# Reordering the first loads and tile preparations of a fused LayerNorm, linear-attention and GELU-MLP kernel

## The chip, the cores and the metric

The kernel runs on one core of a Trainium2 chip. The metric is the device time of one execution in microseconds (us), and I quote medians of several executions. A "span" is the length of one profiled execution, from its first to its last instruction; it is 1.7 to 1.9 us shorter than the time. A load has "landed" when its semaphore is full, which is when the engine that waits for it goes on (quarter 0 of W1 lands at 6.65 us and the matmul that waits for it starts at 6.69); the "pitch" of matmuls is the time from one start to the next. The engines are TensorE (PE in the profile, with its weight loads as PEld), VectorE (DVE), ScalarE (ACT), GpSimd (POOL) and SyncE (SP), which issues most of the DMAs.

## The reference

```python
x = A_x                                    # (1, 2048, 640) bf16
xn = layernorm(x)                          # eps 1e-5, no affine part
# A: linear attention with 32 heads of 20
q, k, v = split(xn @ wqkv)                 # wqkv 640 x 1920
phi = lambda t: where(t > 0, t + 1, exp(t)) + 1e-6
kv = einsum(phi(k), v); z = phi(k).sum(tokens)
attn = (phi(q) @ kv / (phi(q) @ z + 1e-6)) @ wo
# B: MLP
mlp = gelu(xn @ w1 + b1) @ w2 + b2         # w1 640 x 1536
return x + attn + mlp
```

Everything below concerns the first 21 us, in which the kernel computes xn for the first few of 16 tiles of 128 tokens and starts on xn @ w1.

## The kernel before

The kernel records instructions per engine in program order, and adds a semaphore wait wherever data or a buffer demands it. An engine starts its instructions in the order of its own list: in the kernel before ScalarE copies tile 0's second piece at 6.51 us and the bias, which stands behind it in the list, at 6.90. The order in the source text therefore matters only within one engine: moving VectorE work past a TensorE unit in the text leaves both lists as they are.

The opening of the kernel before:

```python
# loads; W1 (640 x 1536) comes in four column quarters of 480 KB, x in tiles of 160 KB
dma_x(0, 1)
dma_w("scalar", b1tmp[:], ...)      # bias, on ScalarE's queue
dma_w1(0, "scalar")                 # quarter 0, on ScalarE's queue
dma_x(1, 1); dma_w1(1); dma_x(2, 1); dma_w1(2); dma_x(3, 1); dma_w1(3)   # SyncE's queue
dma_x(4, 2); dma_x(6, 2); ...
# ... (cut)
filler(10)                          # ten zero matmuls of 512 columns
ln_stats(0)                         # VectorE: statistics of tile 0
ln_half(1, 0); ln_half(1, 1); ln_aggr(1)
norm0(0, CA, r_xnA)                 # tile 0 normalised in two pieces: columns 0-255
norm0(CA, D, r_xnB)                 # and 256-639
dA, sA, bA = transp0(0, 2, r_xnA)   # TensorE transposes into PSUM
filler(1)
dB, sB, bB = transp0(2, DT, r_xnB)
# VectorE copies the first piece out of PSUM, ScalarE the second
b1_step()                           # bias transposed on TensorE, copied by ScalarE
ln_norm(1)
h_first([0, 1, 2])                  # first useful matmuls: quarter 0, first piece then second
# ... (cut)
xnT_copy(1, transp(1))
ln_stats(2)
ln_next(2)                          # statistics of tile 3, THEN norm of tile 2
units(0, 1, 3, 2 * JQ)              # units(t0, n, lo, hi): n tiles of tokens, 128-column
units(1, 1, 0, 2 * JQ)              # blocks lo..hi-1 of W1; JQ = 3 blocks are a quarter
units(0, 2, 2 * JQ, 2 * JQ + 2)
xnT_copy(2, transp(2))
units(0, 2, 2 * JQ + 2, JT)
ln_next(3)
ln_next(4)
units(2, 1, 0, JQ)
xnT_copy(3, transp(3))
units(2, 1, JQ, JT)                 # one tile wide: matmuls of 128 columns
units(3, 1, 0, JT)
# tiles 4 to 15 are transposed by DMA; then units of 2 and 4 tiles
```

A normalisation is a chain over three engines: statistics (VectorE, two halves), aggregate (VectorE), the power -0.5 (GpSimd), normalise (VectorE), transpose (TensorE), copy (VectorE or ScalarE). A "unit" means five accumulating matmuls and one GELU.

## Time and profile before

| | before |
|---|---|
| time, median of 3 | 210.07 us (209.99 to 210.41) |
| span of the profiled execution | 207.9 us |
| TensorE busy | 203.1 us, 98% |
| granted TensorE clock | 1.000 |

Part 1 of the page gives busy time and share by engine; part 4 gives the engines' shares of the chain that ended last.

```profile
PE 203.1 (98%) x1592; PEld 140.4 (68%) x1598; DVE 108.1 (52%) x226; ACT 74.3 (36%) x141; POOL 21.1 (10%) x59
...
PE 91%; DVE 4%; DMA 3%; issue 1%; ACTq 0%; DVEq 0%
```

TensorE is the bottleneck nearly throughout. The start of the chain, in order of time (start, length, what), says what TensorE waited for first:

```profile
1.45 5.20 DMA W<-in_B_w_dram
6.65 0.05 issue
6.69 1.04 PE ps L382 x15
7.74 0.28 PE ps L336 x5
8.02 3.60 PE ps L352 x55
11.62 0.28 PE ps L336 x5
11.90 3.02 PE ps L352 x35
```

W1's quarter 0 is issued at 1.45 us and lands at 6.65; from then on the chain is TensorE without a break (the lines behind 14.92 us are cut). The timeline of TensorE for the same stretch (start, length, engine, line, operation, tiles, form, count, and idle time before it with what ended it) shows the same from the engine's side:

```profile
5.72 0.28 PE L372 MATMUL ps<-ident,xn_tm 128*128 128x128 bf16 x2 [0.57 <-DVE xn_tm L365]
5.84 0.38 PE L295 MATMUL ps<-warm 128*128 128x512 bf16 x1
6.14 0.34 PE L372 MATMUL ps<-ident,xn_tm 128*128 128x128 bf16 x3
6.41 0.18 PE L300 MATMUL ps<-ident,b1tmp 12*128 12x12 bf16 x1
6.69 1.04 PE L382 MATMUL ps<-xnT,W 128*128 128x128 bf16 x15
7.57 0.44 PE L336 MATMUL ps<-ident,xn_tm 128*128 128x128 bf16 x5
7.85 3.77 PE L352 MATMUL ps<-xnT,W 128*128 128x128 bf16 x55
```

L382 is the first useful matmul. L336 are the transposes of tiles 1 to 3. Behind 7.57 no idle time is noted: a change of this stretch can pay only by starting TensorE's work earlier or by making it shorter.

### The profile page before, as it was taken

The numbers are of one execution on the slowest core, as the hardware profiler recorded it, in microseconds if no ns is written. First come the engines' busy times: TensorE is split into PE (matmuls) and PEld (weight loads), VectorE is DVE, ScalarE is ACT, GpSimd is POOL, SyncE is SP. The second block draws the span as 40 slices with busy tenths as digits, with TensorE's granted clock in tenths as the row PEclk, the third lists the DMA queues.
The fourth block names the chain that finished last, engine by engine and source line by source line (L and its number), as shares of the span: only waits on it lengthen the run. The fifth ranks groups of instructions, "written<-read, shape, count | busy, mean of one in ns | idle before, by whom it ended". The sixth has DMA issues, their size and how long they took to land.

```text
span 207.9 us, 3963 instructions
## 1 busy us (share of the span) xinstructions
PE 203.1 (98%) x1592; PEld 140.4 (68%) x1598; DVE 108.1 (52%) x226; ACT 74.3 (36%) x141; POOL 21.1 (10%) x59
## 2 busy tenths in 40 slices
PE   7899999999999999999999999999999999999995
PEld 2799886444457777777756565577777777777775
DVE  4689960000008888998268865474863422523322
ACT  2689887666676445111153577100000000000000
POOL 3245567000041000000000000000000000000000
PEclk9999999999999999999999999999999999999999
DMA  5999779997000000000000000681111111001001
GB/s 167 343 358 110 119 123 152 372 324 249 3 0 0 0 3 0 0 3 0 0 3 2 0 3 0 202 309 47 71 59 57 63 39 54 32 32 35 32 34 62
DMA packets 22698, 17.98 MB, mean 86 GB/s; under 512 B 9240, under 2 KB 22680, under 8 KB 22680
## 3 DMA queue, kind: packets, MB, share of 16 engines
q1 hardware_dynamic: 22000, 17.24, 29.5%
q10 hardware_dynamic: 680, 0.49, 0.9%
q8 instruction: 12, 0.20, 0.4%
q14 instruction: 6, 0.05, 0.1%
HBM read 12.62 MB, written 2.62 MB: 73 GB/s over the span
## 4 chain that ended last, share of the span: by engine, by line
PE 91%; DVE 4%; DMA 3%; issue 1%; ACTq 0%; DVEq 0%
PE ps L612 33%; PE ps L352 25%; PE ps L511 10%; PE ps L473 10%; PE ps L523 7%; DVE PQ L463 3%; DMA W<-in_B_w_dram 3%; PE ps L648 2%; DVE ek L461 1%; PE ps L532 1%; PE ps L548 1%; PE ps L558 1%; PE ps L382 1%; PE ps L336 0%; ACTq L233 0%
## 5 line engine op out<-in xcount | busy, mean ns | idle before, releaser
L352 PE MATMUL ps<-xnT,W 128*128 128x128 bf16 (+2 forms) x432 | 51.8, 281 | 0.2
L612 PE MATMUL ps<-W,HG 128*128 128x320 bf16 x360 | 51.0, 299 | 0.0
L352 PEld LDWEIGHTS ps<-xnT,W 128*128 128x128 bf16 x435 | 35.5, 98 | 15.6
L612 PEld LDWEIGHTS ps<-W,HG 128*128 128x128 bf16 x360 | 35.1, 98 | 14.2 <-issue 0.4
L356 ACT ACTIVATE HG<-ps,b1c 128x128 bf16<-128x128 f32 (+2 forms) x87 | 40.0, 492 | 12.5 <-PE ps L352 10.3
L461 DVE TENSOR_SCALAR ek<-ek 128x512 bf16<-128x512 bf16 (+1 forms) x36 | 11.1, 308 | 41.7 <-ACT ek L460 40.5
L460 ACT ACTIVATE ek<-ps 128x512 bf16<-128x512 f32 (+1 forms) x36 | 23.2, 644 | 19.8 <-PE ps L523 10.1
L631 DVE TENSOR_TENSOR out_sb<-ps,xnT 128x640 bf16<-128x640 f32 x15 | 12.4, 825 | 33.5 <-PE ps L612 33.3
L612 PE MATMUL ps<-Msb,PQ 128*128 128x320 bf16 x150 | 22.3, 299 | 0.0
L511 PE MATMUL ps<-xPK,xn_tm 128*128 128x320 bf16 x160 | 22.1, 299 | 0.0
L473 PE MATMUL ps<-Wqkv,xnT 128*128 128x320 bf16 x160 | 21.9, 299 | 0.0
L523 PE MATMUL ps<-xnT,Wqkv 128*128 128x512 bf16 x97 | 21.4, 379 | 0.3 <-issue 0.2
L473 PEld LDWEIGHTS ps<-Wqkv,xnT 128*128 128x128 bf16 x160 | 15.6, 98 | 6.3
L511 PEld LDWEIGHTS ps<-xPK,xn_tm 128*128 128x128 bf16 x160 | 15.6, 98 | 6.0
L612 PEld LDWEIGHTS ps<-Msb,PQ 128*128 128x128 bf16 x150 | 14.6, 98 | 5.7
L523 PEld LDWEIGHTS ps<-xnT,Wqkv 128*128 128x128 bf16 x100 | 11.6, 118 | 9.6 <-ACT Msb L553 0.2
L463 DVE SCALAR_TENSOR_TENSOR PQ<-ps,ek 128x512 bf16<-128x512 f32 x20 | 13.8, 692 | 2.1
L308 DVE BATCH_NORM_STATS2 stats<-xPK 128x6 f32<-128x320 bf16 x32 | 13.6, 466 | 2.5 <-DMA xPK<-in_A_x_dram 2.4
L463 DVE SCALAR_TENSOR_TENSOR xPK<-ps,ek 128x640 bf16<-128x640 f32 x16 | 13.2, 825 | 1.7
L498 DVE TENSOR_TENSOR Msb<-Msb,xPK 128x640 f32<-128x640 f32 x14 | 11.6, 826 | 0.5
L515 ACT ACTIVATE W<-ps 128x640 bf16<-128x640 f32 x5 | 3.5, 703 | 18.6 <-PE ps L511 18.6
L318 POOL TENSOR_TENSOR rstd<-aggr,mhalf 128x1 f32<-128x1 f32 x16 | 9.1, 568 | 8.9 <-DVE aggr L316 8.9
(62 smaller groups left out, 90.6 us busy)
## 6 DMA issues: line engine op xcount, KB each, us to landing
xnT<-in_A_x_dram SPq DMA_DIRECT2D x4, 640.0 KB, 6.6
Wqkv<-in_A_wqkv_dram SPq DMA_DIRECT2D x3, 800.0 KB, 6.4
out_dram<-out_sb SPq DMA_DIRECT2D x15, 160.0 KB, 1.8
W<-in_B_w_dram SPq DMA_DIRECT2D x1, 1920.0 KB, 15.6
W<-in_B_w_dram SPq DMA_DIRECT2D x3, 480.0 KB, 6.8
xPK<-in_A_x_dram SPq DMA_DIRECT2D x2, 640.0 KB, 9.4
Wo<-in_A_wo_dram SPq DMA_DIRECT2D x1, 800.0 KB, 10.9
xPK<-in_A_x_dram SPq DMA_DIRECT2D x4, 160.0 KB, 4.2
```

The source lines that it names most:

```text
L308: Pl.ins(v, lambda e: e.bn_stats(stats[:, s, 6 * h:6 * h + 6], x_in[:, t, h * HW:(h + 1) * HW]), reads=[r_x[t]], writes=[r_stats[s][h]])
L352: Pl.ins("tensor", [(lambda e, k=k: e.matmul(bank(b, 0, w), W1[:, k, jb * P:(jb + 1) * P], xnT[:, k, tok], start=(k == 0), stop=(k == DT - ...
L356: Pl.ins("scalar", lambda e: e.activation(HG[:, jb, tok], bank(b, 0, w), ACT.Gelu_apprx_tanh, bias=b1c[:, jb:jb + 1]), reads=[B_[b], r_b1c ...
L460: Pl.ins("scalar", lambda e: e.activation(e2, src, ACT.Exp), reads=br, writes=[r_ek[s]])
L461: Pl.ins(v, lambda e: e.tensor_scalar(et, et, 1.0, 1e-6, ALU.min, ALU.add), reads=[r_ek[s]], writes=[r_ek[s]])
L463: Pl.ins(v, lambda e: e.scalar_tensor_tensor(out=d2, in0=src, scalar=0.0, in1=e2, op0=ALU.max, op1=ALU.add), reads=br + [r_ek[s]], writes= ...
L473: fns.append(lambda e, k=k, h=h, b=b, t=t: e.matmul(bank(b + h, 0, HW), xnT[:, k, t * P:(t + 1) * P], Wqkv[:, k, D + h * HW:D + (h + 1) * ...
L498: Pl.ins(v, lambda e, t=t: e.tensor_tensor(out=zsum, in0=zsum, in1=PK[:, t, :], op=ALU.add), reads=[r_PK[t], r_zsum], writes=[r_zsum])
L511: Pl.ins("tensor", [(lambda e, t=t, h=h, b=b, f=f: e.matmul(bank(b + h, 0, HW), xn_tm[:, t, f * P:(f + 1) * P], PK[:, t, h * HW:(h + 1) * ...
L523: Pl.ins("tensor", [(lambda e, k=k, j=j, b=b: e.matmul(bank(b), Wqkv[:, k, j:D:DT], xnT[:, k, cc], start=(k == 0), stop=(k == DT - 1))) fo ...
L612: return lambda e: e.matmul(bank(b + h, 0, HW), l, r[:, h * HW:(h + 1) * HW], start=(i == 0), stop=(i == JT + DT - 1))
L631: Pl.ins(v, lambda e: e.tensor_tensor(out=halves(out_sb[:, s, :]), in0=pair(b), in1=halves(x_res[:, t, :]), op=ALU.add), reads=B_[b:b + 2] ...
```

## The change

The intent: all of the first loads on one queue, in the order in which they are needed, so that quarter 0 is not shared against quarter 1; tile 0's normalisation ahead of tile 1's aggregate; the bias transpose out of the way among the zero matmuls; tile 2's normalisation no longer behind tile 3's statistics; and tiles 2 and 3 together in the second half of W1.

```diff
         dma_x(0, 1)
         dma_w("scalar", b1tmp[:], ...)
-        dma_w1(0, "scalar")
         dma_x(1, 1)
+        dma_w1(0)
         dma_w1(1)
+        dma_w1(2)
         dma_x(2, 1)
-        dma_w1(2)
+        dma_w1(3)
         dma_x(3, 1)
-        dma_w1(3)
 ...
-        filler(10)
+        filler(6)
+        b1_step()
+        filler(3)
         ln_stats(0)
         ln_half(1, 0)
         ln_half(1, 1)
-        ln_aggr(1)
         norm0(0, CA, r_xnA)
         norm0(CA, D, r_xnB)
+        ln_aggr(1)
 ...   (first piece now copied by ScalarE, second by VectorE)
-        b1_step()
         ln_norm(1)
         h_first([0, 1, 2])
 ...
         xnT_copy(1, transp(1))
-        ln_stats(2)
-        ln_next(2)
         units(0, 1, 3, 2 * JQ)
         units(1, 1, 0, 2 * JQ)
-        units(0, 2, 2 * JQ, 2 * JQ + 2)
+        units(0, 2, 2 * JQ, 3 * JQ)
+        ln_stats(2)
+        ln_norm(2)
+        ln_half(3, 0)
+        ln_half(3, 1)
+        ln_aggr(3)
         xnT_copy(2, transp(2))
-        units(0, 2, 2 * JQ + 2, JT)
-        ln_next(3)
+        units(0, 2, 3 * JQ, JT)
+        ln_half(4, 0)
+        ln_norm(3)
+        ln_half(4, 1)
+        ln_aggr(4)
+        units(2, 1, 0, JQ)
+        b3 = transp(3)
+        xnT_copy(3, b3)
+        units(2, 1, JQ, 2 * JQ)
         ln_next(4)
-        units(2, 1, 0, JQ)
-        xnT_copy(3, transp(3))
-        units(2, 1, JQ, JT)
-        units(3, 1, 0, JT)
+        units(3, 1, 0, 2 * JQ)
+        units(2, 2, 2 * JQ, JT)
```

In both kernels tile 1's transposes come right behind the first three units: in that place TensorE's order is the same.

More of the change, by code (lines that the diff above doesn't have):

```diff
@@ L403, in bass_parallel_sum__linear_attn_block__dense_activation_gelu__prompt_kernel @@
         dB, sB, bB = transp0(2, DT, r_xnB)
-        Pl.ins(v, lambda e: e.tensor_copy(dA, sA), reads=[B_[bA]], writes=[r_xnTA])
-        Pl.ins("scalar", lambda e: e.activation(dB, sB, ACT.Copy), reads=[B_[bB]], writes=[r_xnT[0]])
-        b1_step()
+        Pl.ins("scalar", lambda e: e.activation(dA, sA, ACT.Copy), reads=[B_[bA]], writes=[r_xnTA])
+        Pl.ins(v, lambda e: e.tensor_copy(dB, sB), reads=[B_[bB]], writes=[r_xnT[0]])
         ln_norm(1)
```

## The prediction

> **What bounds it now.** TensorE: busy 203.1 of 207.9 us (page, part 1), 91% of the chain that ended last, granted clock 1.000. In time order PE does filler until 5.1 us, waits for the first normalised tile, and starts its first useful matmul at 6.69 us. From 7.06 us to 115 us it never idles. So a change to the first 21 us pays only by what it brings forward PE's work from 7 us on, or makes that work shorter.
>
> **What holds the first matmuls (timeline, tile and DMA views).** W1 quarter 0, alone on ACT's queue, lands at 6.65 us; quarter 1 at 7.66, x2 8.10, quarter 2 9.61, x3 10.07, quarter 3 11.57. Nearly as late are tile 0's transposed halves: VectorE's copy ends at 6.33, ScalarE's at 7.00 (PE stalls a trace there: the second half starts at 7.06).
>
> **What the change does.**
> 1. DMA order. In 4.4-6.2 us both queues moved data together at 343 GB/s (DMA view by queue)[...]. Estimate from the landings: 6.0 us (issued 0.3 us later). Total bytes up to quarter 1 are unchanged, so it still lands at about 7.55. Later steady pace: 480 KB per 1.5 us, 160 KB per 0.45. So x2 moves back, to about 9.5 (was 8.10), x3 to 11.5 (was 10.07).
> 2. Tile 0. Its normalisation no longer waits behind tile 1's aggregate (0.27 us earlier); swapped copies: halves ready at about 6.2 and 6.6. First matmul about 6.25, second half 6.63 instead of 7.06: -0.43 us. The bias transpose (0.18 us) leaves a PE gap, worth nothing by itself.
> 3. Six 256-wide units replace twelve 128-wide ones. PE's pitch is 55.9 ns at 128 columns, 109.2 ns at 256: 60x55.9-30x109.2 = 0.08 us saved. ScalarE was within its pace: nothing.
> 4. VectorE work is reordered: tile 2 no longer waits for x3; norm(4) moves behind the third copy, so tile 4's DMA transpose goes out near 16.9 us (was 15.08), tile 5's near 18.2 (was 16.90), landing near 20.9 (was 19.49).
>
> **How much reaches PE.** The 0.43 is taken back in turns. Quarter 1 is needed at 7.41 and lands near 7.55: 0.25 left. Tile 2's transposes come up at about 11.75; from x2's landing through stats, aggregate, power and normalisation to PE is 2.46 us by the durations of tiles 0 and 1, so 9.5 gives about 11.97: a stall of 0.2, gain about zero. The later steps have slack. The merge leaves about 0.1. Tile 5's transpose lands at about the time (20.8-20.9) when PE asks for it, so up to 0.2 may go there. From there the program is the same.
>
> **Prediction.** 209.95 us, range 209.3 to 210.6. Faster by over 2%: 0.01; within 2%: 0.98; slower by over 2%: 0.01.
>
> **What would show it.** Step 1: landings of quarter 0 near 6.0, quarter 1 7.4-7.7, x2 9.3-9.7. Step 2: first useful matmul 6.2-6.3, its second half near 6.63. Gain taken back: small PE idle before the first 128-wide unit (DMA W) and before tile 2's transposes (VectorE xn_tm), and perhaps before the first unit of tiles 4-5 (DMA transpose). Step 3: that unit starts within 0.3 us of the earlier 20.90. The end, PE chain and DVE-bound stretch at 115-123 us, unchanged.
>
> **What would make it wrong.** If one queue fills the slow stretch at 2.8-4.3 us (213 GB/s), all loads land up to 0.5 us sooner and the gain of 0.4-0.5 survives. If quarter 0 lands after 6.6, or tile 5's transpose runs into the long stall that tile 6's showed (4.7 us to landing against 2.6), it loses 0.5-1.5 us.

The 6.0 us is quarter 0's landing, and an estimate: it takes quarter 0 to be through before quarter 1 starts, which no trace had shown. The sum is that of "How much reaches PE": of the 0.43 us 0.25 are left at quarter 1 and about none at tile 2's transposes; the merge brings about 0.1, and tile 5's transpose may take up to 0.2. It comes to about 0.1 us under the 210.07 of the kernel before, the 209.95 predicted.

## The result, and the profile after

| | before | after |
|---|---|---|
| time, median | 210.15 us (209.99 to 210.50, 6 runs) | 209.97 us (209.82 to 210.37, 6 runs) |
| ratio, 95% interval | | 0.9991 (0.9978 to 1.0004) |
| span of the profiled execution | 207.9 us | 208.5 us |
| granted TensorE clock | 1.000 | 1.000 |

A ratio is the mean time of one kernel's fast runs over that of the other's in the same rounds, so it is not quite the ratio of the medians. The time did not change clear of noise. The profiled span is 0.6 us longer than before, although the medians are 0.18 us shorter. The runs' own times settle most of that: the profiled execution of the kernel before took 209.68 us, less than all six runs of its median, and that of the changed kernel 210.37 us, the longest of its six.

Part 1 of the page, and TensorE's timeline of the changed kernel:

```profile
PE 204.2 (98%) x1567; PEld 139.7 (67%) x1567; DVE 108.5 (52%) x226; ACT 73.9 (35%) x135; POOL 21.4 (10%) x59
```

```profile
5.40 0.40 PE L372 MATMUL ps<-ident,xn_tm 128*128 128x128 bf16 x2
5.58 0.46 PE L295 MATMUL ps<-warm 128*128 128x512 bf16 x1
5.88 0.33 PE L372 MATMUL ps<-ident,xn_tm 128*128 128x128 bf16 x3
6.60 1.01 PE L382 MATMUL ps<-xnT,W 128*128 128x128 bf16 x15 [0.39 <-DMA W<-in_B_w_dram]
7.45 0.44 PE L336 MATMUL ps<-ident,xn_tm 128*128 128x128 bf16 x5
8.11 4.32 PE L352 MATMUL ps<-xnT,W 128*128 128x128 bf16 x60 [0.22 <-DMA W<-in_B_w_dram]
12.50 0.45 PE L336 MATMUL ps<-ident,xn_tm 128*128 128x128 bf16 x5
```

Tile 0's transposes start 0.3 us earlier (5.40 against 5.72) and its last ones 0.26 us earlier (5.88 against 6.14), but TensorE then waits for quarter 0 until 6.60, and behind tile 1's transposes for quarter 1 until 8.11. The timeline rounds such waits by the modelled ends of matmuls; by the starts, 0.38 us are lost ahead of 8.11, 0.23 ahead of 12.50, and 0.16 ahead of the first 256-wide unit of tiles 4 and 5 (a matmul's start less that of the one before it, less the usual pitch of 56 ns at 128 columns or 109 at 256). The chain that ended last names the middle one:

```profile
3.33 6.68 DMA xPK<-in_A_x_dram
10.01 0.02 issue
10.04 0.90 DVE stats L308 x2
...
11.03 0.22 DVE aggr L316
...
11.32 0.58 POOL rstd L318
...
12.00 0.46 DVE xn_tm L329
12.45 0.05 issue
12.50 0.45 PE ps L336 x5
```

x2 lands at 10.01 us, and the normalisation behind it takes 2.49 us to reach TensorE. This is a true critical path through a small tile of x that the new queue order had put behind 1.4 MB of weights.

Landings and TensorE's milestones in ten of the fourteen traces, in us from the span's start, read from the issue records and instruction starts of each trace ("start 45" is the first 256-wide unit of tiles 4 and 5; from there on all versions issue the same work on TensorE; no_filler, sched_warm, q0_first and q0_b1_late are left out):

| trace | quarter 0 | quarter 1 | x2 | x3 | first useful matmul | start 45 | tile 5's DMA transpose |
|---|---|---|---|---|---|---|---|
| before | 6.65 | 7.66 | 8.10 | 10.07 | 6.69 | 20.90 | 19.49 |
| before_again | 6.33 | 7.53 | 7.98 | 9.92 | 6.91 | 21.27 | 19.85 |
| merge_only | 6.99 | 7.86 | 8.36 | 10.28 | 7.04 | 21.14 | 19.77 |
| compute_only | 7.37 | 7.60 | 8.07 | 10.03 | 7.42 | 23.20 | 23.11 |
| after | 6.56 | 8.06 | 10.01 | 11.95 | 6.60 | 21.50 | 21.41 |
| after_again | 6.42 | 7.90 | 9.88 | 11.83 | 6.46 | 21.37 | 21.28 |
| dma_only | 6.08 | 7.60 | 9.57 | 11.50 | 6.78 | 22.27 | 20.84 |
| x2_early | 6.20 | 7.68 | 8.15 | 11.57 | 6.33 | 20.88 | 20.79 |
| sched | 6.52 | 7.95 | 8.44 | 10.36 | 6.57 | 20.97 | 20.27 |
| sched_again | 6.56 | 7.93 | 8.40 | 10.32 | 6.61 | 20.96 | 20.24 |

### The profile page after: what moved, and what is told of

Its sections match the earlier page's. It is cut to its first block, busy times and chain, and to the rows that moved or that the text cites. A ratio compares the mean times of both kernels' runs of the same rounds, so it can differ in the third digit from the quotient of the medians.

```text
span 208.5 us, 3901 instructions
## 1 busy us (share of the span) xinstructions
PE 204.2 (98%) x1567; PEld 139.7 (67%) x1567; DVE 108.5 (52%) x226; ACT 73.9 (35%) x135; POOL 21.4 (10%) x59
## 4 chain that ended last, share of the span: by engine, by line
PE 89%; DVE 5%; DMA 3%; SPq 1%; issue 1%; POOL 0%; DVEq 0%
PE ps L621 33%; PE ps L352 23%; PE ps L520 10%; PE ps L482 10%; PE ps L532 7%; DMA xPK<-in_A_x_dram 3%; DVE PQ L472 3%; PE ps L657 2%; DVE ek L470 1%; PE ps L541 1%; SPq L233 1%; PE ps L557 1%; PE ps L567 1%; DVE stats L308 0%; SPq L229 0%
## 5 line engine op out<-in xcount | busy, mean ns | idle before, releaser
L352 PE MATMUL ps<-xnT,W 128*128 128x256 bf16 (+2 forms) x405 | 52.1, 290 | 0.2 <-DMA W<-in_B_w_dram 0.2
L356 ACT ACTIVATE HG<-ps,b1c 128x256 bf16<-128x256 f32 (+2 forms) x81 | 39.5, 510 | 13.6 <-PE ps L352 11.2
L470 DVE TENSOR_SCALAR ek<-ek 128x512 bf16<-128x512 bf16 (+1 forms) x36 | 11.0, 307 | 40.4 <-ACT ek L469 39.3
L532 PE MATMUL ps<-xnT,Wqkv 128*128 128x512 bf16 x100 | 22.1, 379 | 0.0
L580 DVE TENSOR_TENSOR PQ<-PQ,ek 128x512 bf16<-128x512 bf16 x20 | 7.0, 419 | 6.0 <-DMA ek<-rden 6.0
```

Of the source, the lines that this page charges most:

```text
L352: Pl.ins("tensor", [(lambda e, k=k: e.matmul(bank(b, 0, w), W1[:, k, jb * P:(jb + 1) * P], xnT[:, k, tok], start=(k == 0), stop=(k == DT - ...
L356: Pl.ins("scalar", lambda e: e.activation(HG[:, jb, tok], bank(b, 0, w), ACT.Gelu_apprx_tanh, bias=b1c[:, jb:jb + 1]), reads=[B_[b], r_b1c ...
L470: Pl.ins(v, lambda e: e.tensor_scalar(et, et, 1.0, 1e-6, ALU.min, ALU.add), reads=[r_ek[s]], writes=[r_ek[s]])
L532: Pl.ins("tensor", [(lambda e, k=k, j=j, b=b: e.matmul(bank(b), Wqkv[:, k, j:D:DT], xnT[:, k, cc], start=(k == 0), stop=(k == DT - 1))) fo ...
```

## The experiments

Twelve runs were made, in three batches of four; a batch shares its chip, its rounds and its runs of the kernel before, and each batch had another chip, so times are best compared within a batch. All were correct. My theory from the prediction: the earlier start is real, and is taken back by the landings of quarter 1 and x2 and then by tile 5's DMA transpose. Rivals: the DMA order is neutral; or the compute order earns and the DMA order loses; or all of it is off the path.

### before_again: the kernel before, unchanged

> The kernel before, unchanged: the noise floor and a second trace. Ratio to before 1.000 within 0.002. The first trace has W1 quarter 0 landing at 6.65 us, the first useful matmul at 6.69 and the first 256-wide unit of tiles 4 and 5 at 20.90; its span (207.9) was short for this kernel. If the 0.6 us by which the changed kernel's profiled span was longer is luck of the profiled executions, this trace should start that unit later than 20.90, by up to 0.3 us; if it is the change's, this trace repeats 20.90.

Measured: 210.09 us (5 runs), ratio 0.9997 (0.9984 to 1.0010). "Start 45" is at 21.27 us, not 20.90. The chain of this execution begins elsewhere:

```profile
1.25 4.45 PE ps L295 x10
5.70 0.01 issue
5.71 0.39 PE ps L372 x2
6.11 0.43 PE ps L295
6.53 0.32 PE ps L372 x3
6.85 0.12 PE ps L300
6.97 1.14 PE ps L382 x15
```

Here quarter 0 had landed at 6.33, and TensorE itself was the limit. The starts of successive matmuls say why: in this execution 128-column matmuls follow at 107 ns until about 7.0 us, and at 56 ns only later. In the first trace the pitch had halved by about 4.6 us: its zero matmuls of 512 columns follow at 427 ns up to 4.2 us, and the last two start 217 ns apart, at 4.55 and 4.77. So the 0.6 us by which the changed kernel's profiled span was longer is mostly luck, on both sides: the first trace of the kernel before was one of its good executions, and that of the changed kernel was its slowest. The expectation "by up to 0.3 us later" was a little short (0.37).

### dma_only: the new DMA order, old compute order

```diff
-        dma_w1(0, "scalar")
-        dma_x(1, 1); dma_w1(1); dma_x(2, 1); dma_w1(2); dma_x(3, 1); dma_w1(3)
+        dma_x(1, 1); dma_w1(0); dma_w1(1); dma_w1(2); dma_x(2, 1); dma_w1(3); dma_x(3, 1)
```

> The new DMA order alone, old compute order. Theory (landings take the gain back): quarter 1 near 8.05, x2 near 10.0, x3 near 11.95. The old VectorE order puts tile 3's statistics ahead of tile 2's normalisation, so tile 2's transposes wait for x3: 11.97 + 0.8 + 0.45 is about 13.2 instead of 11.46, a loss of 1.5 to 1.9 us in all: 211.6 to 212.1, ratio 1.007 to 1.009. Rival (DMA order is neutral, the start is set by the copies of tile 0): within 0.3 us of before.

Measured: 211.10 us, ratio 1.0041 (1.0029 to 1.0053), a loss of 0.9 us against the 210.22 of its rounds. The trace has the forecast mechanism, a gap of 1.10 us ahead of tile 2's transposes, which start at 12.82 us behind x3's landing at 11.50, and no other new gap behind it. The forecast of 1.5 to 1.9 us was too large: the landings were 0.4 us earlier than assumed, and it was counted from the lucky first trace. The rival that the DMA order is neutral falls: on its own it costs, and the compute order of the change is what makes it bearable.

### compute_only: the new compute order, old DMA order

```diff
-        dma_x(1, 1); dma_w1(0); dma_w1(1); dma_w1(2); dma_x(2, 1); dma_w1(3); dma_x(3, 1)
+        dma_w1(0, "scalar")
+        dma_x(1, 1); dma_w1(1); dma_x(2, 1); dma_w1(2); dma_x(3, 1); dma_w1(3)
```

> The new compute order with the old DMA order. Theory: the first matmul still waits for quarter 0 (6.65), so it starts at 6.65 to 6.70; its second half no longer waits (7.03 instead of 7.06); no wait for quarter 1 or x2; the first unit of tiles 4 and 5 starts at 20.75 to 20.95, held by tile 5's transpose. Gain 0.0 to 0.15 us: 210.0, ratio 0.9993 to 1.000. Rival (the compute part earns and the DMA order loses): gain of 0.4 us or more, ratio below 0.998.

Measured: five of six runs 210.26 to 210.47, one 212.11, median 210.28; ratio 1.0016 (0.9990 to 1.0041). So the compute part alone does not earn 0.4 us; the rival falls, and the forecast of 210.0 is missed by 0.3, within the interval. The profiled execution is the one of 212.11 us, and shows something that none of my theories had. Three stretches of 1 us in it (the columns are start:end, length, PE busy with the number of matmuls, granted clock, DMA share, GB/s):

```profile
8.40:9.40 1.00, 1.00 (x12) 1.00 1.09 338
9.40:10.40 1.00, 1.00 (x13) 1.00 1.10 332
11.00:12.00 1.00, 1.00 (x22) 1.00 1.07 360
```

and the same two first stretches of the kernel before:

```profile
8.40:9.40 1.00, 1.00 (x22) 1.00 1.08 337
9.40:10.40 1.00, 1.00 (x22) 1.00 1.09 330
```

TensorE is busy all the time in both and the granted clock reads 1.00 in both, but the one does half as many 128-column matmuls in a microsecond. Their pitch is 107 ns until 10.7 us, then 56. In this execution quarter 0 landed at 7.37 and TensorE had stood still from about 6.6 to 7.4. In these traces the pitch falls from 107 to 56 ns at another moment each time: at about 4 us (sched_again), 4.6 (before), 5.6 (after), 7.0 (before_again) and 10.7 (compute_only). In the twelve traces that have a clock record, the record begins only where the pitch changes (at 4.11, 4.45, 5.74, 7.01 and 10.64 us in these five), and the views print 1.00 where nothing is recorded. So a granted clock of 1.00 says nothing of a kernel's first microseconds here. What sets the moment of the change is not shown.

### x2_early: the changed kernel with x2 ahead of quarter 2

```diff
         dma_w1(1)
-        dma_w1(2)
         dma_x(2, 1)
+        dma_w1(2)
         dma_w1(3)
```

> The changed kernel with x2 issued between quarters 1 and 2 instead of behind quarter 2. Theory (x2's landing sets tile 2's transposes): x2 lands near 8.5 instead of 10.0, the stall of 0.28 us ahead of tile 2's transposes goes, and everything behind it moves up together: first unit of tiles 4 and 5 about 0.2 to 0.3 us earlier than in the changed kernel, time about 209.7. Rival (PE is held later anyway, by tile 5's DMA transpose): stall gone but the unit starts at the same time, within 0.1 us, and the time is unchanged.

Measured: 210.07 us, ratio 0.9990 (0.9978 to 1.0002), no different from the changed kernel's 0.9991. In the trace the theory's first half holds: x2 lands at 8.15, and the gap ahead of tile 2's transposes is gone (0.23 us before). "Start 45" is at 20.88, and a gap of 0.17 us is still ahead of it, for tile 5's DMA transpose, which landed at 20.79. Two things kept that from the time. The first matmul of this trace was 0.27 us earlier than in the changed kernel's, which is the landing of quarter 0, ahead of the edit in the queue; and 0.27 us were lost again between 144.6 and 150.3 us, where TensorE's work took 5.70 us instead of the 5.43 us of the kernel before. This second loss shows in the traces of x2_early, sched, no_filler, after_again and q0_first, by 0.18 us in compute_only, and by 0.02 us or not at all in the others, so it seems to go with the execution and not with the version. The traces show what it waits for. There TensorE needs PQ, which VectorE scales with the reciprocals of the denominators, and these come back in broadcasts of 32 KB (`ek<-rden`). A broadcast usually lands 1.9 us behind its issue; in x2_early the third took 3.6 us and the fourth, on which the scaling waits, landed at 143.99 instead of 143.03. Behind that, TensorE follows VectorE at 0.34 us for two matmuls that otherwise take 0.27. The loss is largest in no_filler, where the fourth took 3.77 us and landed at 145.29 (timelines of VectorE and of TensorE):

```profile
145.41 1.77 DVE L578 TENSOR_TENSOR PQ<-PQ,ek 128x512 bf16<-128x512 bf16 x5 [5.78 <-DMA ek<-rden]
145.89 5.86 PE L619 MATMUL ps<-Msb,PQ 128*128 128x320 bf16 x40 [0.51 <-DVE PQ L578]
```

In all fourteen traces a packet of 16 KB on the DMA queue that the profile calls "instruction" falls between the issue and the landing of the first broadcast that is late (in the changed kernel's first trace issue at 140.81, packet at 141.77, landing at 144.10); that it is the cause was not tested.

### no_filler: the changed kernel without its nine opening zero matmuls

```diff
-        filler(6)
         b1_step()
-        filler(3)
```

> The changed kernel without the nine zero matmuls that open it (the bias transpose and the one zero matmul between tile 0's transposes stay). Theory (the start also hangs on TensorE's clock: matmuls follow at 107 ns per 128 columns[...], then at 56): the first useful matmuls follow at 107 ns until 10 to 12.5 us, half of that stretch is lost, less the 0.6 us of waits for quarter 1 and x2 that it hides: 1.0 to 2.5 us slower than the changed kernel, ratio to before 1.004 to 1.011. Rival (the pitch doubled in the compute_only trace for another reason, e.g. contention with the loads): the pitch is 56 ns from the first useful matmul on and the time is within 0.3 us of the changed kernel.

The 10 to 12.5 us and the loss worked out from them are no more than a guess; compute_only's trace, which was at hand, had the slow pitch until 10.7 us.

Measured: 212.00 us (4 runs, 211.37 to 212.38), ratio 1.0090 (1.0074 to 1.0106). The rival falls as to the pitch: the loads are the same, and the first useful matmul of the trace starts at 6.46, as early as with the zero matmuls, but matmuls follow at 107 ns until 8.24 (the clock record begins at 8.29). The forecast time holds too, but the trace does not show the theory behind it. "Start 45" is at 21.57 us, only 0.07 later than in the changed kernel's first trace and 0.20 later than in its second: the slow matmuls cost about 0.8 us (an estimate: nearly half of the 1.78 us from 6.46 to 8.24), and the waits for quarter 1 and x2, which are gone, give 0.6 back. The larger loss of this execution, 0.94 us, is the late broadcast at 145 us shown above. It is the fastest of the four (211.37), and the others have no trace. So the kernel without the nine zero matmuls, which compute nothing, took 2.0 us or 1% more than the kernel before in the same rounds; that the slow pitch at the start makes up those 2 us is not shown.

### sched: loads and VectorE work in the order of need

```diff
         dma_w1(1)
-        dma_w1(2)
         dma_x(2, 1)
-        dma_w1(3)
+        dma_w1(2)
         dma_x(3, 1)
+        dma_w1(3)
 ...
         ln_stats(2)
-        ln_norm(2)
         ln_half(3, 0)
+        ln_norm(2)
         ln_half(3, 1)
 ...
         b3 = transp(3)
+        ln_half(5, 0)
+        ln_half(5, 1)
         xnT_copy(3, b3)
         units(2, 1, JQ, 2 * JQ)
-        ln_next(4)
+        ln_norm(4)
+        ln_aggr(5)
```

> The changed kernel with x2 ahead of quarter 2 and x3 ahead of quarter 3 (all on one queue), tile 5's statistics ahead of the third copy, and tile 4's normalisation right behind it. Theory (the gain is taken back by x2's landing and then by tile 5's transpose): no PE gap ahead of tile 2's transposes, none ahead of the first unit of tiles 4 and 5; that unit starts at 20.5 to 20.8 when the clock is fast by the first matmul; 0.3 to 0.5 us under the changed kernel: about 209.6, ratio 0.997. Rival (a few tenths gained here are lost later, as they were in the x2_early trace at 145 to 150 us): gaps gone, time within 0.15 us of the changed kernel, ratio 0.999.

Measured: 209.79 us (5 runs, 209.50 to 210.22), ratio 0.9984 (0.9971 to 0.9997); so clear of the kernel before, but by 0.2 to 0.3 us. Both gaps are gone: tile 2's transposes and "start 45" follow the matmul ahead of them without a pause. The trace is of the slowest of the five runs (210.22) and has the late loss of x2_early's, 0.37 us here. What remains is the start, 6.57 us for quarter 0 and 0.30 us lost at quarter 1, so "start 45" came at 20.97 instead of the 20.5 to 20.8 expected.

### q0_first: sched with quarter 0 issued first, on ScalarE's queue

```diff
         dma_x(0, 1)
+        dma_w1(0, "scalar")
         dma_w("scalar", b1tmp[:], ...)
         dma_x(1, 1)
-        dma_w1(0)
         dma_w1(1)
```

> The kernel of the run sched with quarter 0 alone on ACT's queue, issued there before the bias instead of behind it (0.80 instead of 1.73 us). Theory (quarter 0's landing starts PE): quarter 0 lands at 5.6 to 6.0, quarter 1 at 7.0 to 7.4, x0 up to 0.3 us later than 3.1; first useful matmul 6.2 to 6.5; the wait for quarter 1 shrinks below 0.1; 0.1 to 0.35 us under sched, about 209.35, ratio 0.996. Rival (the two queues share the DMA engines, so quarter 0 is not served sooner by being issued sooner, and x0 is held up): quarter 0 after 6.2, first matmul not before 6.6, time equal to sched or above.

That the two queues share the DMA engines shows in the trace of the kernel before: of the 16 engines' time, as the DMA view counts it, SyncE's queue took 108.4% on its own (6.6 to 13.4 us), ScalarE's 72.4% beside 20.0% of SyncE's (2.8 to 4.3 us), and later the two took 65.2% and 39.3% (SyncE's and ScalarE's, 4.4 to 6.2 us).

Measured: 212.03 us, ratio 1.0099 (1.0079 to 1.0118). Quarter 0 landed at 4.92 us, much earlier than either theory had it, and quarter 1 at 6.90; and still the first useful matmul came at 8.05. x1, issued at 1.25 on the other queue, landed at 5.42 instead of the 3.5 to 4.1 of the traces in which quarter 0 is issued later. The DMA view of 2.5 to 4.1 us by queue (packets, MB, share of 16 engines' time; q10 is ScalarE's queue, q1 SyncE's) shows how little SyncE's queue moved beside quarter 0:

```profile
q10 hardware_dynamic: 539, 0.41, 79.9%
q1 hardware_dynamic: 81, 0.08, 16.4%
```

The 81 packets of q1 are still x0's: in the packet records x1's first packet starts at 4.16 us, when 560 of quarter 0's 640 packets had ended (4.17). VectorE has tile 1's statistics ahead of tile 0's normalisation in its list, so that late x1 held up tile 0 (its first piece starts at 6.24 us instead of 4.99). The bias also landed late, so that TensorE stood at its transpose from about 4.0 to 5.7 us, and matmuls followed at 107 ns until 10.2. Issuing quarter 0 earlier made x0 (3.39 us instead of 3.04 in sched), x1 and the bias later; the loads behind them came earlier, quarter 1 at 6.90 instead of 7.95 and x2 at 7.38 instead of 8.44. An order that keeps this and has x0 and x1 first was not tried.

### q0_b1_late: q0_first with the bias transpose moved behind tile 0's transposes

```diff
-        filler(6)
-        b1_step()
-        filler(3)
+        filler(9)
 ...
         dB, sB, bB = transp0(2, DT, r_xnB)
+        b1_step()
```

> The kernel of the run q0_first (212.03) with the bias transpose moved from among the opening zero matmuls to behind tile 0's transposes. Theory (of its 2.2 us loss the larger part was TensorE standing at the bias transpose for a bias that now lands behind quarter 0, and the slow clock that this left until 10.2 us; the rest is tile 0's normalisation standing behind tile 1's statistics for x1): no wait at 3.7 to 5.7 us, first useful matmul near 7.2 at 56 ns, 210.2 to 210.8. Rival (the loss comes from x0 and x1 landing later): 211.5 to 212.1.

Measured: 212.70 us (211.08 to 214.06), ratio 1.0116 (1.0070 to 1.0163). The forecast of 210.2 to 210.8 failed. The wait at the bias did go, but the trace shows that my edit had made a new one: in ScalarE's list the bias copy (8.19 us) now stood ahead of the copy of tile 0's first piece (8.27), so the first useful matmul came at 8.79; and with TensorE idle from about 5.3 to 6.9 us, matmuls still followed at 107 ns up to 14.0 us. How q0_first's 2.2 us divide between the bias, x1 and the slow pitch stays open. That x1's late landing holds up tile 0 is in both traces (its first piece is normalised at 6.24 and 6.51).

### merge_only: twelve narrow units merged into six wide ones in the kernel before

```diff
-        units(2, 1, JQ, JT)
-        units(3, 1, 0, JT)
+        units(2, 1, JQ, 2 * JQ)
+        units(3, 1, 0, 2 * JQ)
+        units(2, 2, 2 * JQ, JT)
```

> The kernel before, with only the twelve 128-wide units of tiles 2 and 3 (second half of W1) merged into six 256-wide ones. Both theories: PE's time from the end of tile 3's transposes to the first unit of tiles 4 and 5 shrinks from 5.86 to 5.79 us, 0.08 us; no new gap. The look has no timing fine enough for that; it also adds a trace of the old start: quarter 0 at 6.3 to 7.4.

Measured: one look, 209.86 us. From the end of tile 3's transposes to "start 45" it is 21.14-15.35 = 5.79 us, against 20.90-15.04 = 5.86 in the kernel before, with no new gap: 0.07 to 0.08 us, as computed. No timing here could resolve it. Quarter 0 landed at 6.99 in this trace.

### after_again and sched_again: the changed kernel and sched, in the same rounds

> The changed kernel, unchanged, on the same chip and in the same rounds as the next three: ratio to before 0.998 to 1.000. A second trace of it: gaps ahead of the first unit after tile 1's transposes (quarter 1), ahead of tile 2's transposes (x2) and ahead of the first unit of tiles 4 and 5 (tile 5's transpose) again, of 0.1 to 0.4 us each, unless the clock is slow at the first matmul, in which case the first two are hidden under slow matmuls.

> The kernel of the run sched again, beside the changed kernel. Theory: 0.1 to 0.4 us under the changed kernel of the same rounds (209.6 to 209.8), no gap ahead of tile 2's transposes or of the first unit of tiles 4 and 5. Rival (the 0.3 us of the run sched were luck): within 0.1 us of the changed kernel.

Measured: after_again 210.42 us (6 runs, 210.14 to 210.74), ratio 1.0002 (0.9967 to 1.0036); sched_again 209.80 us (6 runs, 209.42 to 210.05), ratio 0.9971 (0.9940 to 1.0003). The intervals are wide because one of the eleven runs of the kernel before took 212.24 us. Beside each other the two sets do not overlap: the mean of sched_again is 209.79, that of after_again 210.44, ratio 0.9969. The gaps in after_again's trace are those of the first one: 0.36 us at quarter 1, 0.26 ahead of tile 2's transposes, 0.17 at tile 5's transpose. After_again's ratio of 1.0002 is just above the expected 0.998 to 1.000. TensorE's timeline of sched_again:

```profile
6.61 1.01 PE L382 MATMUL ps<-xnT,W 128*128 128x128 bf16 x15 [0.42 <-DMA W<-in_B_w_dram]
7.46 0.44 PE L336 MATMUL ps<-ident,xn_tm 128*128 128x128 bf16 x5
7.98 4.32 PE L352 MATMUL ps<-xnT,W 128*128 128x128 bf16 x60
12.14 0.44 PE L336 MATMUL ps<-ident,xn_tm 128*128 128x128 bf16 x5
12.41 2.64 PE L352 MATMUL ps<-xnT,W 128*128 128x256 bf16 x30
14.89 0.44 PE L336 MATMUL ps<-ident,xn_tm 128*128 128x128 bf16 x5
15.17 7.04 PE L352 MATMUL ps<-xnT,W 128*128 128x128 bf16 x85
```

Against the changed kernel's timeline above, the row at 7.98 ends where the transposes of tile 2 begin (the row's length includes the modelled end of the last matmul), and the last row runs on into the units of tiles 4 and 5. So the two waits were on TensorE's path, and removing them pays: "start 45" is 0.41 us earlier than in after_again, out of 0.62 us between the medians. A further 0.27 us of after_again's span is the late broadcast between 145 and 151 us that some executions have; so of the 0.62 us not all is the edit. Sched beats the changed kernel in the one batch in which both ran. Against the kernel before it is 0.2 us faster, clear of noise, in one batch, and 0.3 us, with an interval that just reaches 1, in the other.

### sched_warm: sched with short zero matmuls in two of the waits

```diff
         dB, sB, bB = transp0(2, DT, r_xnB)
+        filler(4, P)      # four zero matmuls of 128 columns
 ...
         xnT_copy(1, transp(1))
+        filler(4, P)
```

> The kernel of sched with four zero matmuls of 128 columns behind tile 0's last transposes and four behind tile 1's, where TensorE waits for quarters 0 and 1. Theory[...]: the slow stretch past 7 us is seen more rarely, the highest of the runs falls by some tenths, the median by 0 to 0.2 us against sched. Rival (these few matmuls[...] delay the real ones): median equal or up to 0.2 us higher.

Measured: 210.22 us (6 runs, 209.54 to 211.24), ratio 0.9996 (0.9959 to 1.0032). The theory's forecast failed: the highest run did not fall but rose (211.24 us, against 210.05 in sched_again). This agrees better with the rival, though the spread of runs is too wide to say that the additions cost something. In its trace the pitch fell to 56 ns at about 6.4 us and "start 45" came at 20.99, as in sched.

## Why the prediction was right or wrong

The predicted time, 209.95 us within 209.3 to 210.6, held (209.97), and so did the main statement, that an earlier start is taken back by waits and the time stays. Its terms fared unequally.

- **Waits that take the gain back: right.** All three named places show a gap in both traces of the changed kernel: quarter 1 (0.38 and 0.36 us), tile 2's transposes (0.23 and 0.26; predicted 0.2), tile 5's DMA transpose (0.16 and 0.17; predicted up to 0.2). That they are on the path, sched shows by taking the last two away.
- **The chain from x2 to TensorE: right.** Predicted 2.46 us from x2's landing to its transposes, measured 12.50-10.01 = 2.49.
- **Landings: wrong by half a microsecond in these two traces.** Quarter 0 was predicted at 6.0, and landed at 6.56 and 6.42; quarter 1 at 7.55, landed at 8.06 and 7.90; x2 at 9.5, landed at 10.01 and 9.88. In six other traces with quarter 0 behind x1 on the one queue it landed at 6.08 to 6.56. The estimate took away the sharing with quarter 1, but up to 4.50 us there was hardly any: by then 351 of quarter 0's 640 packets had ended and 3 of quarter 1's in the trace before, and again 351 in the trace after. Only behind that did the queues share (262 packets of ScalarE's and 211 of SyncE's between 4.5 and 5.5 us). Nor did one queue fill the slow stretch that the prediction named: 204 GB/s in 2.8 to 4.3 us, against 213 before. Nor was quarter 0 through before quarter 1 started: in the trace after 868 packets of the weights' 768 bytes had started by 5.61 us, 228 more than quarter 0 has. In the packet records of this trace quarter 0 ends in 16 packets of 4 bytes: 14 of them are there by 5.12 us, the last two at 5.61 and 6.06, and the semaphore is full at 6.56. In the trace before the last is at 6.16 and the semaphore full at 6.65. So in both traces the landing followed the last of these 16 packets, by 0.5 us, rather than the mean rate. Why two of them came late stays open.
- **First matmul and second half: wrong by 0.2 to 0.35 us in the same sense.** Predicted 6.25 and 6.63; the first matmul came at 6.60 and 6.46, and the second half at 6.95 and 6.81. Tile 0's halves were in time (normalisation 0.37 us earlier, 4.99 against 5.37); quarter 0 was not.
- **The starting point: wrong, and this partly hid the error above.** "Start 45" was predicted within 0.3 us of 20.90, and came at 21.50 and 21.37 in the traces. But 20.90 was one execution whose pitch had halved early, by 4.6 us; the same kernel's second trace has 21.27. The prediction took one profiled execution for the kernel, and did not consider that landings and the pitch of the first 7 us move the start by several tenths from execution to execution (first useful matmul at 6.69, 6.91 and 7.04 in three traces of the old start). So an error of some 0.4 us in the kernel before and one of the same sense in the changed kernel cancelled in the forecast of the time, and that part is luck. How large the second one is stays open: both traces of the changed kernel are of executions slower than their median. An estimate: the traces without the late broadcast have 187.0 us of span behind "start 45", and with it up to 0.4 us more (0.94 in no_filler). The runs beside the median of 209.97 us have spans of 208.1 us, so their "start 45" lies near 21.1 at the latest, inside the predicted 0.3 us; those beside the median of after_again have 208.5 and 208.7, which gives 21.5 to 21.7 at the latest.
- **Merging units: right.** 0.08 us predicted, 0.07 to 0.08 measured in merge_only.
- **Two queues moving data together: right only in part.** Between 4.4 and 6.2 us both queues moved data, as the prediction read from the trace (343 GB/s; 65.2% of the 16 engines' time for SyncE's queue, 39.3% for ScalarE's). But in q0_first x1's first packet starts at 4.16 us, when 560 of quarter 0's 640 packets had ended. Why the one queue stood back there is not shown by any run here.

## What to carry to other kernels

Order loads by when the chain behind them must be done, not by size or by when the data is read: x2, of 160 KB, needed 2.5 us of normalisation behind its landing, and putting it behind 480 KB of weights more cost 0.2 to 0.3 us of waiting in the traces. When an early start is gained, walk on to every later point at which the engine meets a transfer, because a gain survives only down to the next landing that did not move: here, of 0.32 us gained at tile 0's first transposes (5.40 against 5.72), 0.09 were left at the first useful matmul behind quarter 0's landing (6.60 against 6.69). For effects of tenths of a microsecond at a kernel's start take several traces of the same kernel first, and look up where each profiled execution lies among the times of the runs: here the first trace of the kernel before was of a faster execution than any timed, and that of the changed kernel of the slowest. Check the pitch of the first matmuls too. In compute_only's trace a wait of 0.8 us for quarter 0 came with a slow pitch up to 10.7 us, and that execution took 1.8 us more than the median.
